# Filter rows interleaved over SBUF partitions, and x and the filter loaded by two queues on opposite halves

## The chip, the cores and the metric

The kernel runs on one core of a Trainium2 chip. The metric is the device time of one execution in microseconds; lower is better. An execution of the kernel before takes 2681.92 us (median of three, 2678.74 to 2682.32). "TensorE", "VectorE", "ScalarE", "GpSimd" (also POOL) and "SyncE" (also SP) are the core's engines; PE, PEld, DVE, ACT, POOL and SPq are their rows in the profile. DMAs are issued from SyncE, ScalarE (hardware queues) or GpSimd (the software queue).

## The reference

A spectral filter over the sequence axis, followed by a two-layer network with an ELU in between:

```python
batch, seq, dim = (8, 3008, 256)          # filt_r, filt_i: (1505, 256), float32
X = np.fft.rfft(x, axis=1)
F = (filt_r + 1j * filt_i)[None, :, :]
y = np.fft.irfft(X * F, n=x.shape[1], axis=1).astype(np.float32)

h = y.reshape(24064, 256) @ w_in          # w_in (256, 2048), double precision in DRAM
g = np.where(h > 0.0, h, np.exp(np.minimum(h, 0.0)) - 1.0)
out = (g @ w_out).astype(np.float32)      # w_out (2048, 256), double precision in DRAM
```

## The kernel before

The transform of length 3008 is split as 47 x 64. The first factor (64 points, `a_unit`, for batch 0 `a_first`) multiplies x by a twiddled table; the second (47 points, `b_unit`, L302) transforms over the other index with the tables `gb`/`gf` and multiplies by the filter on VectorE (L312 to L315); `bi_unit` (L325) goes back over the 47 points with `gr` and `gi`, `y_write`/`y_read` turn the layout through DRAM, and `n_unit` (L356) does the inverse 64 points and leaves the rows of y in SBUF. The network follows per group of rows: `up_steps` (h and the ELU, L411 to L433) and `down_steps` (L493), both by a scheme of seven products instead of eight.

The order is written out by hand (`tc.manual_schedule()`, L633): each engine executes its instructions, and each queue issues its DMAs, in program order. After a start-up for batch 0, a plan (L715 to L776) interleaves the network of one batch with the transforms of the next. The change lies in the start-up, and in the one-time arrangement of the filter in DRAM for batches 1 to 7.

The start-up has these parts:

- `w_fetch(k)`, k = 0 to 15 (L546): one 512 KB piece of the double-precision weights, on the GpSimd queue, into a borrowed buffer. `w_split` (VectorE), `w_float` (ScalarE) and `w_join` (VectorE) turn it into float32. `tick(k)` is `w_float(k)` and `w_join(k - 1)`.
- `x_load_first(c)`, c = 0 to 5 (L212): a twiddle table `tf` of 256 KB over 128 partitions, four rows per x position to partitions 0 to 63 (pieces of 4 KB), and the mirrored rows to partitions 64 to 127 (pieces of 1 KB). All three are on the sync queue.
- `a_first(c)` (L231) multiplies them and evicts to `zt`; `t_first(g)` (L246) transposes back.
- `f_read_first(ff, a, part)` (L280): the filter for batch 0 into `ff`, a tile of 128 partitions by 8 groups. Part 0 is `filt_r` on the sync queue, part 1 `filt_i` on the GpSimd queue; `a` is the half of the partitions (from 0, or from 64). In each half, rows 0 to 23 are the ascending frequencies (one transfer of 384 KB), rows 24 to 46 the mirrored ones, descending (each `u` in a transfer of 16 rows and one of 7, up to 128 and 56 KB). Row 24 to 47 of group 0 has one more transfer (L295).
- The loop over c (L667) splits, converts and joins weight c, runs `a_first(c)`, and fetches weight c + 2 once a one-element GpSimd copy (`junk`, L670) has seen x part c arrive.
- The loop over g = 0 to 9 (L688) is the filter stage: `b_unit` for group g, `bi_unit` and `y_write` for g - 2, and one weight by `TICKS`. At its end come the first `y_read` and `n_unit(0, 0)` (L711).

`f_arrange` (L615) later copies both filters into a DRAM tile `fd` whose rows lie as those of `ff`; `f_read` loads one group of it as 48 + 48 whole rows for the batches after the first.

Of the kernel before, what the change touches and what calls it, by code (L numbers as in the profile page):

```python
# [22 lines left out]
N1 = 47  # L23
# [17 lines left out]
def _make_tables():  # L41

    n2, k2 = np.arange(N2), np.arange(K2)
    ta, tn = np.zeros((P, H, P)), np.zeros((P, H, P))
    for i in range(H):
        for h in range(2):
            if h and i == 0:
                continue
            n1 = N1 - i if h else i
            th = 2 * np.pi * (((N1 * n2[:, None] + n1) * k2[None]) % N) / N  # L60
            c, s = np.cos(th), -np.sin(th)
            c[:, 0], s[:, 0] = 1.0, 1.0 - 2.0 * (n2 % 2)
            sign = -1.0 if h else 1.0
            r = slice(h * 64, h * 64 + 64)
            for p, v in enumerate((c, sign * s, s, sign * c)):
                ta[r, i, p * 32:p * 32 + 32] = v
                tn[p * 32:p * 32 + 32, i, r] = v.T
    tf = np.ascontiguousarray(ta.reshape(P, H, 4, K2).transpose(0, 1, 3, 2)).reshape(P, H, P)
    tb = ta.reshape(2, 2, 32, NXC, 2, 2, 4, 16, 2)[:, 0].transpose(3, 0, 1, 2, 4, 7, 5, 6)
    ta = np.ascontiguousarray(tb).reshape(P, H // 2, P)  # L70
    i = np.arange(H)[:, None]
    gb, gr, gi = (np.zeros((P, 2, 64)) for _ in range(3))
    q = np.arange(N1)[None]
    th = 2 * np.pi * ((i * np.where(q < 24, q, 70 - q)) % N1) / N1
    c, s = np.cos(th), np.sin(th)
    sign = np.where(q < 24, 1.0, -1.0)
    gb[0:24, 0, :N1], gb[24:48, 0, :N1] = c, s
    gb[64:88, 0, :N1], gb[88:112, 0, :N1] = c * sign, -s * sign
    for o in (0, 64):
        gr[o:o + N1, 0, 0:24], gr[o:o + N1, 0, 24:48] = 2 / N * c.T, 2 / N * s.T  # L80
        gi[o:o + N1, 0, 0:24], gi[o:o + N1, 0, 24:48] = 2 / N * (c * sign).T, -2 / N * (s * sign).T
    k1 = np.arange(24)[None]
    t0 = 2 * np.pi * ((i * k1) % N1) / N1
    t3 = 2 * np.pi * ((i * (32 + 64 * k1)) % N) / N
    c0, s0, c3, s3 = np.cos(t0), np.sin(t0), np.cos(t3), np.sin(t3)
    gb[0:24, 1, 0:24], gb[24:48, 1, 24:48] = c0, c3
    gb[64:88, 1, 24:48], gb[88:112, 1, 0:24] = -s3, -s0

    m0, m3 = np.full((24, 1), 2 / N), np.full((24, 1), 2 / N)
    m0[0] = m3[23] = 1 / N  # L90
    s0[:, 0] = s3[:, 23] = 0.0
    gr[0:24, 1, 0:24], gr[24:48, 1, 24:48] = m0 * c0.T, m3 * c3.T
    gi[0:24, 1, 24:48], gi[24:48, 1, 0:24] = -m0 * s0.T, -m3 * s3.T
    gf = np.zeros_like(gb)
    for o in (0, 64):
        gf[o:o + 48] = gb[o:o + 48].reshape(2, H, 2, 64).swapaxes(0, 1).reshape(48, 2, 64)
    return [t.astype(np.float32) for t in (ta, tn, gb, gr, gi, tf, np.eye(P), gf)]
# [8 lines left out]
def kernel(  # L106
# [39 lines left out]
    w_in, w_out = ([glob.tile([P, 7, 2, P], FP32, name="%s%d" % (n, i)) for i in range(4)] for n in ("wi", "wo"))  # L146

    fbufs = [glob.tile([P, 2, 2, D], FP32, name="f%d" % i) for i in range(FBUFS)]
    junk = glob.tile([P, 1], FP32, name="junk")
    edges = glob.tile([P, 2], FP32, name="edges")  # L150
    fd = fdp.tile([NG, 2, 48, 2, 2, D], FP32, name="fd")

# [2 lines left out]
    def raw(src, row, ap, col=0):  # L155
        return bass.AP(tensor=src.tensor, offset=src.offset + row * D + col, ap=ap)
# [52 lines left out]
    zt = [[], [w[3].rearrange("p a b c -> p (a b c)") for w in (w_in, w_out)]]  # L209
    ROWS = 112  # L210

    def x_load_first(c):  # L212
        if c < XBUFS:
            t = xp.tile([P, 2, 2, D], FP32, tag="xc", name="xc").rearrange("p k u d -> p (k u) d")
        else:
            t = t1p.tile([P, XC, D], FP32, tag="t1", name="x1")
        if c < 2:
            w = tnp.tile([P, 4, P], FP32, tag="tn", name="tn")
        else:
            if c % 2 == 0:  # L220
                tas["pair"] = t4p.tile([P, 4, D], FP32, tag="t4", name="t0").rearrange("p u (w f) -> p (u w) f", f=P)
            w = tas["pair"][:, 4 * (c % 2):4 * (c % 2) + 4, :]
        xs[0, c], tas[0, c] = t, w
        nc.sync.dma_start(w, tf_d[:, 4 * c:4 * c + 4, :])
        nc.sync.dma_start(t[HALVES[0]].rearrange("p u d -> p (u d)"), raw(x, XC * c, [[N1 * D, 64], [1, XC * D]]))
        u = 1 if c == 0 else 0
        if u:
            nc.gpsimd.memset(t[HALVES[1], 0, :], 0.0)
        nc.sync.dma_start(t[HALVES[1], u:XC, :], raw(x, N1 - XC * c - u, [[N1 * D, 64], [-D, XC - u], [1, D]]))

    def a_first(c):  # L231
        xt, w = xs.pop((0, c)), tas.pop((0, c))
# [44 lines left out]
        for a, r in enumerate((LO, HI)):  # L277
            nc.gpsimd.dma_start(t[r].rearrange("p c u d -> p (c u d)"), fd[g, a].rearrange("q c u d -> q (c u d)"))

    def f_read_first(t, a, part):  # L280

        r = a * 64
        for src, c, queue in (((filt_r, 0, nc.sync), (filt_i, 1, nc.gpsimd))[part],):
            queue.dma_start(t[r:r + 24, :, c, :, :].rearrange("q g u d -> q g (u d)"),
                                raw(src, 2 * a, [[64 * D, 24], [4 * D, NG], [1, 2 * D]]))
            for u in range(2):
                g0 = 1 if a == u == 0 else 0
                for r0, n in ((24, 16), (40, 7)):  # L290
                    queue.dma_start(t[r + r0:r + r0 + n, g0:NG, c, u, :],
                                        raw(src, 64 * (r0 - 23) - 4 * g0 - 2 * a - u,
                                            [[64 * D, n], [-4 * D, NG - g0], [1, D]]))
            if a == 0:
                queue.dma_start(t[24:48, 0, c, 0, :], raw(src, 32, [[64 * D, 24], [1, D]]))  # L295

    def tile_mm(ps, table, k, rhs, special):
        for u, w, v in ((0, 1, 1), (1, 1, 0)) if special else ((0, 2, 0),):
# [316 lines left out]
    def f_arrange():  # L615

        for c, src in enumerate((filt_r, filt_i)):
            for a in range(2):
                nc.gpsimd.dma_start(fd[:, a, 0:24, c, :, :].rearrange("g q u d -> q g (u d)"),
                                    raw(src, 2 * a, [[64 * D, 24], [4 * D, NG], [1, 2 * D]]))  # L620
                for u in range(2):
                    g0 = 1 if a == u == 0 else 0
                    nc.gpsimd.dma_start(fd[g0:NG, a, 24:47, c, u, :].rearrange("g q d -> q g d"),
                                        raw(src, 64 - 4 * g0 - 2 * a - u,
                                            [[64 * D, 23], [-4 * D, NG - g0], [1, D]]))

                g0 = 0 if a else 1
                nc.gpsimd.dma_start(fd[g0:NG, a, 47, c, :, :].rearrange("g u d -> g (u d)"),
                                    raw(src, 4, [[2 * D, NG - g0], [1, 2 * D]]))
            nc.gpsimd.dma_start(fd[0, 0, 24:48, c, 0, :], raw(src, 32, [[64 * D, 24], [1, D]]))  # L630
            nc.gpsimd.dma_start(fd[0, 0, 47:48, c, 1, :], raw(src, 4, [[D, 1], [1, D]]))

    with tc.manual_schedule():  # L633


        TICKS = {1: 8, 2: 9, 3: 10, 4: 11, 5: 12, 7: 13, 8: 14, 9: 15}
        with tc.tile_pool(name="boot", bufs=1) as bp:
            ff = bp.tile([P, NG, 2, 2, D], FP32, name="ff")
            eye = bp.tile([P, P], FP32, name="eye")
# [1 line left out]
            pq = [bp.tile([P, 2, D], FP32, name="pq%d" % i) for i in range(2)]  # L641
            zt[0] += [bp.tile([P, 16 * ROWS], FP32, name="zt%d" % i) for i in range(2)]

            for k in range(2):
                w_fetch(k)
            for c in range(NXC):
                x_load_first(c)
            wtmp.append([kp.tile([P, 512], U32, tag=t, name=n) for t, n in (("k0", "wm"), ("k1", "we"))] +
                        [kp.tile([P, 2, 512], FP32, tag="c", name="wfl")])
            wtmp.append([sdp.tile([P, 2, D], FP32, tag="sd", name=n).bitcast(U32).rearrange("p a b -> p (a b)")  # L650
# [1 line left out]
                        [t1p.tile([P, XC, D], FP32, tag="t1", name="wfl").rearrange("p (a b) d -> p a (b d)", a=2)])  # L652
            for i, v in enumerate((1151.0 * 2 ** 23, 255.0 * 2 ** 23)):
                nc.vector.memset(edges[:, i:i + 1], v)
            for z in zt[0] + zt[1]:
                nc.gpsimd.memset(z.rearrange("p (k r) -> p k r", r=ROWS)[:, :, 48:64], 0.0)
            nc.gpsimd.memset(ff, 0.0)
            for t, d in ((gr, gr_d), (gi, gi_d), (gf, gf_d), (eye, eye_d)):
                nc.sync.dma_start(t, d)
            for a in range(2):  # L660
                f_read_first(ff, a, 0)

            def tick(k):
                w_float(k)
                w_join(k - 1)

            for c in range(NXC):  # L667
                w_split(c)

                nc.gpsimd.tensor_copy(out=junk[0:1], in_=xs[0, c][0:1, 0, 0:1])  # L670
                w_fetch(c + 2)
                w_float(c)
                a_first(c)
                if c > 0:
                    w_join(c - 1)
            for a in range(2):
                f_read_first(ff, a, 1)
            for k in range(NXC + 2, 14):
                w_fetch(k)
            for g in range(4):  # L680
                t_first(g)
            for k in range(NXC, 8):
                w_split(k)
                tick(k)
                w_fetch(8 + k)
            nc.sync.dma_start(gb, gb_d)
            tn_read(0, 0)
            for g in range(NG + 2):  # L688
# [12 lines left out]
                    y_read(0, 0, (nc.sync, nc.scalar))  # L701
                if k:
                    tick(k)
        w_join(15)
        for c in range(2):
            x_load(1, c)
# [102 lines left out]
```

## Time and profile before

| What | Value |
|---|---|
| Time, median of three | 2681.92 us (2678.74 to 2682.32) |
| Span of the profiled execution | 2675.4 us |
| Busy share: PE, PEld, DVE, ACT, POOL | 97%, 83%, 69%, 56%, 9% |
| DMA rate, 0 to 30 us / 30 to 74 us | 235 / 192 GB/s, share of the DMA engines 0.97 / 1.02 |
| DVE busy, 0 to 30 / 30 to 74 / 74 to 126 us | 12.87 / 13.46 / 47.74 us |
| PE busy, 126 to 2675 us | 2533.72 of 2549 us |

The first row is from timed executions, the others from one profiled execution. The span is cut into stretches of time, and for each the busy time of every engine, the granted TensorE clock, the share of the 16 DMA engines that was occupied and the bytes per second are given. An engine that is full in a stretch bounds it; where none is and the DMA share is near 1, transfers do. In a timeline a row shows start, length, engine, line, operation, result and operands, and in brackets how long the engine was idle before it and what ended that.

### The profile page before, as it was taken

Reading aid. Unit: us, or ns where it says so; the run is one execution under the profiler, and the core shown is the slowest. Engines: PE = TensorE matmul, PEld = TensorE weight load, DVE = VectorE, ACT = ScalarE, POOL = GpSimd, SP = SyncE. Lnnn points to the kernel's source line nnn. Section 1 sums busy time; section 2 is a strip of 40 time slices with the busy share of each in tenths; the row PEclk is TensorE's granted clock in tenths of the full one; section 3 lists DMA queues with packets and bytes.
Section 4 is the critical chain, followed back from the end, with each engine's and each line's share of the span. In section 5 each row is a group of like instructions: output and inputs, shape, how many; then the busy total and the mean of one; then the engine's idle time right before and its main releaser. Section 6 shows DMA issues by size and latency. Waiting matters only on the chain.

```text
span 2675.4 us, 37291 instructions
## 1 busy us (share of the span) xinstructions
PE 2597.6 (97%) x13508; PEld 2213.8 (83%) x13508; DVE 1841.1 (69%) x3201; ACT 1504.4 (56%) x2621; POOL 252.2 (9%) x302
## 2 busy tenths in 40 slices
PE   3699999999999999999999999999999999999998
PEld 3388789887898878988789878898789887898887
DVE  3876766767766776767766776676767677666665
ACT  4565555655555555555555555555555555555554
POOL 3030200012000120002100021000210011000000
PEclk7799999999999999999999999999999999999999
DMA  9564421343114331343314233133421233110110
GB/s 194 145 143 100 112 50 38 90 104 97 38 45 120 86 85 35 82 104 79 77 43 102 73 97 75 38 85 97 103 56 38 73 83 85 38 40 19 22 26 16
DMA packets 230936, 202.87 MB, mean 76 GB/s; under 512 B 132952, under 2 KB 197579, under 8 KB 230753
## 3 DMA queue, kind: packets, MB, share of 16 engines
q1 hardware_dynamic: 213457, 164.84, 25.5%
q0 software_dynamic: 16992, 35.19, 5.5%
q8 instruction: 107, 1.75, 0.3%
q14 instruction: 76, 0.62, 0.1%
q10 hardware_dynamic: 304, 0.46, 0.1%
HBM read 128.45 MB, written 74.97 MB: 76 GB/s over the span
## 4 chain that ended last, share of the span: by engine, by line
PE 95%; DMA 3%; DVE 2%; ACT 0%; issue 0%; SPq 0%; POOL 0%; DVEq 0%; POOLq 0%; ACTq 0%
PE po L493 42%; PE phs L411 25%; PE phd L411 12%; PE pha L411 6%; PE psn L363 3%; PE pva L300 2%; PE psr L300 2%; PE psa L201 2%; DMA wd<-in_moe_w_out_dram 1%; DMA ff<-in_filt_i_dram 1%; DMA xc<-in_x_dram 1%; DMA tn<-tf_t 0%; PE pvb L300 0%; PE psa L236 0%; PE psi L300 0%
## 5 line engine op out<-in xcount | busy, mean ns | idle before, releaser
L493 PE MATMUL po<-g,wo 128*128 128x256 f32 (+1 forms) x5376 | 1297.1, 376 | 0.0
L493 PEld LDWEIGHTS po<-g,wo 128*128 128x128 f32 x5376 | 1016.7, 190 | 127.9 <-issue 16.2
L422 ACT ACTIVATE g<-phs 128x512 f32<-128x512 f32 (+1 forms) x576 | 338.7, 588 | 843.3 <-PE phs L411 842.6
L419 DVE TENSOR_TENSOR g<-phd,g 128x512 f32<-128x512 f32 (+1 forms) x384 | 259.4, 676 | 464.9 <-ACT e L429 278.7
L429 ACT ACTIVATE e<-e 128x512 f32<-128x512 f32 (+1 forms) x768 | 477.3, 621 | 24.3
L411 PE MATMUL phs<-y,wi 128*128 128x256 f32 (+1 forms) x1536 | 395.0, 380 | 0.0
L411 PE MATMUL phs<-ys,wi 128*128 128x256 f32 (+1 forms) x1536 | 387.8, 375 | 1.5 <-ACT g L422 1.5
L433 DVE SCALAR_TENSOR_TENSOR g<-e,g 128x512 f32<-128x512 f32 (+1 forms) x576 | 386.9, 672 | 0.2 <-ACT e L429 0.2
L428 ACT ACTIVATE e<-g 128x512 f32<-128x512 f32 (+1 forms) x576 | 352.9, 613 | 35.1 <-DVE g L419 29.0
L411 PEld LDWEIGHTS phs<-y,wi 128*128 128x128 f32 x1536 | 285.0, 190 | 82.7 <-ACT t L332 34.1
L411 PEld LDWEIGHTS phs<-ys,wi 128*128 128x128 f32 x1536 | 291.9, 190 | 34.8 <-ACT g L422 2.2
L433 DVE SCALAR_TENSOR_TENSOR g<-e,phs 128x512 f32<-128x512 f32 (+1 forms) x192 | 129.9, 677 | 138.4 <-ACT e L429 138.4
L411 PE MATMUL phd<-ys,wi 128*128 128x256 f32 (+1 forms) x768 | 194.0, 375 | 1.8 <-DVE g L419 1.8
L411 PE MATMUL pha<-y,wi 128*128 128x256 f32 (+1 forms) x768 | 193.9, 375 | 0.0
L411 PE MATMUL phd<-y,wi 128*128 128x256 f32 (+1 forms) x768 | 193.7, 375 | 0.0
L428 ACT ACTIVATE e<-phs 128x512 f32<-128x512 f32 (+1 forms) x192 | 112.9, 588 | 141.9 <-PE phs L411 141.0
L321 POOL TENSOR_TENSOR sr<-sr,sp 128x512 f32<-128x512 f32 x56 | 71.2, 1271 | 1242.8 <-DVE sp L314 1242.8
L411 PEld LDWEIGHTS phd<-ys,wi 128*128 128x128 f32 x768 | 145.9, 190 | 18.7 <-DVE g L419 2.5
L411 PEld LDWEIGHTS pha<-y,wi 128*128 128x128 f32 x768 | 146.0, 190 | 16.6 <-ACT y L365 0.2
L411 PEld LDWEIGHTS phd<-y,wi 128*128 128x128 f32 x768 | 146.1, 190 | 16.2
L473 DVE TENSOR_TENSOR g<-g,g 128x512 f32<-128x512 f32 (+1 forms) x192 | 130.7, 681 | 6.7
L470 DVE TENSOR_TENSOR g<-g,g 128x512 f32<-128x512 f32 (+1 forms) x192 | 130.7, 681 | 6.6
(141 smaller groups left out, 2403.0 us busy)
## 6 DMA issues: line engine op xcount, KB each, us to landing
yd<-t SPq DMA_DIRECT2D x127, 192.0 KB
t<-yd SPq DMA_DIRECT2D x190, 128.0 KB
z<-t SPq DMA_DIRECT2D x84, 256.0 KB
f<-fd POOLq DMA_DIRECT2D x112, 192.0 KB, 3.7
t<-z SPq DMA_DIRECT2D x224, 96.0 KB
out_dram<-o SPq DMA_DIRECT2D x640, 32.0 KB
tn<-tn_t SPq DMA_DIRECT2D x48, 256.0 KB
xc<-in_x_dram SPq DMA_DIRECT2D x84, 128.0 KB
```

The costliest lines, as they stand in the source:

```text
L300: nc.tensor.matmul(ps[:, u:u + w, :], table[k, v, :], r[k, u:u + w, :], start=n == 0, stop=n == len(rhs) - 1)
L321: nc.gpsimd.tensor_tensor(out=sr, in0=sr, in1=p, op=ALU.add)
L363: nc.tensor.matmul(ps[:, ts(q, P)], t[:, i - 4 * m, ds(dh * P, P)], w[:, i - 4 * m, :], start=True, stop=True)
L411: nc.tensor.matmul(ps[:, a, 0:h], w_in[q][:, COMBO[n], a, :], y[n], start=start and a == 0, stop=True, skip_group_check=True)
L419: nc.vector.tensor_tensor(out=g[o], in0=i0, in1=i1, op=ALU.add)
L422: nc.scalar.activation(out=g[o], in_=i0, func=AXT.Copy)
L428: nc.scalar.activation(out=e, in_=src, func=AXT.Relu, scale=-1.0)
L429: nc.scalar.activation(out=e, in_=e, func=AXT.Exp, scale=-1.0)
L433: nc.vector.scalar_tensor_tensor(out=g[n], in0=es[n], scalar=1.0, in1=src, op0=ALU.subtract, op1=ALU.max)
L470: nc.vector.tensor_tensor(out=b12, in0=b22, in1=b12, op=ALU.subtract)
L473: nc.vector.tensor_tensor(out=g["t4"], in0=g["b21"], in1=g["t2"], op=ALU.subtract)
L493: nc.tensor.matmul(po[i][:, u, 0:h], w_out[q][:, COMBO[n], a, :], g[n][:, a, :], start=q == 0 and a == 0 and n in (1, 3, 6, 4), stop=True, ...
```

## The change

It is meant to [...]keep two queues on opposite halves of the partitions at the same time. It has four parts:

1. In each half the filter's rows are interleaved: ascending frequencies on the even rows, mirrored ones on the odd rows. The rows and columns of the tables (`gb`, and with it `gf`, `gr`, `gi`) are permuted to fit, and so is the DRAM copy for the later batches.
2. x's upper rows go to the GpSimd queue, its lower rows and the twiddles stay on the sync queue. The filter's real part (sync) takes the lower half first, the imaginary part (GpSimd) the upper half first.
3. The order of the start-up: x and the weights 0 to 4 are issued in turn from the beginning, without the `junk` copies; the imaginary filter is issued after weight 6; weight 7 is converted in the filter stage at g = 0 and no longer ahead of it.
4. The zero fill of `ff` is split between ScalarE and VectorE, where GpSimd did it alone; that of one x row moves from GpSimd to VectorE.

```diff
@@ tables
+    lie = np.concatenate([2 * np.arange(24), 2 * np.arange(24) + 1])
+    gb[:, :, lie] = gb[:, :, :48].copy()
+    for t in (gr, gi):
+        for o in (0, 64):
+            t[o + lie] = t[o:o + 48].copy()
@@ x_load_first
         xs[0, c], tas[0, c] = t, w
-        nc.sync.dma_start(w, tf_d[:, 4 * c:4 * c + 4, :])
+        if c == 0:
+            nc.vector.memset(t[HALVES[1], 0, :], 0.0)
+
+    def x_load_first(c):
+        t = xs[0, c]
+        u = 1 if c == 0 else 0
         nc.sync.dma_start(t[HALVES[0]].rearrange("p u d -> p (u d)"), raw(x, XC * c, [[N1 * D, 64], [1, XC * D]]))
-        u = 1 if c == 0 else 0
-        if u:
-            nc.gpsimd.memset(t[HALVES[1], 0, :], 0.0)
-        nc.sync.dma_start(t[HALVES[1], u:XC, :], raw(x, N1 - XC * c - u, [[N1 * D, 64], [-D, XC - u], [1, D]]))
+        nc.gpsimd.dma_start(t[HALVES[1], u:XC, :], raw(x, N1 - XC * c - u, [[N1 * D, 64], [-D, XC - u], [1, D]]))
+        nc.sync.dma_start(tas[0, c], tf_d[:, 4 * c:4 * c + 4, :])
@@ f_read_first
-        for src, c, queue in (((filt_r, 0, nc.sync), (filt_i, 1, nc.gpsimd))[part],):
-            queue.dma_start(t[r:r + 24, :, c, :, :].rearrange("q g u d -> q g (u d)"),
...
+        src, queue = ((filt_r, nc.sync), (filt_i, nc.gpsimd))[c]
+        for a in ((0, 1), (1, 0))[c]:
+            r = a * 64
+            queue.dma_start(t[r:r + 48:2, :, c, :, :].rearrange("q g u d -> q g (u d)"),
...
-                for r0, n in ((24, 16), (40, 7)):
-                    queue.dma_start(t[r + r0:r + r0 + n, g0:NG, c, u, :],
...
+                for j, n in ((0, 16), (16, 7)):
+                    queue.dma_start(t[r + 1 + 2 * j:r + 2 * (j + n):2, g0:NG, c, u, :],
...
             if a == 0:
-                queue.dma_start(t[24:48, 0, c, 0, :], raw(src, 32, [[64 * D, 24], [1, D]]))
+                queue.dma_start(t[1:48:2, 0, c, 0, :], raw(src, 32, [[64 * D, 24], [1, D]]))
@@ f_arrange (its other transfers alike)
-                nc.gpsimd.dma_start(fd[:, a, 0:24, c, :, :].rearrange("g q u d -> q g (u d)"),
+                nc.gpsimd.dma_start(fd[:, a, 0:48:2, c, :, :].rearrange("g q u d -> q g (u d)"),
@@ start-up
-        TICKS = {1: 8, 2: 9, 3: 10, 4: 11, 5: 12, 7: 13, 8: 14, 9: 15}
+        TICKS = {0: 7, 1: 8, 2: 9, 3: 10, 4: 11, 5: 12, 7: 13, 8: 14, 9: 15}
...
-            for k in range(2):
-                w_fetch(k)
+            for z in zt[0] + zt[1]:
+                nc.gpsimd.memset(z.rearrange("p (k r) -> p k r", r=ROWS)[:, :, 48:64], 0.0)
+            for c in range(NXC):
+                x_place_first(c)
             for c in range(NXC):
                 x_load_first(c)
+                if c < 5:
+                    w_fetch(c)
+            nc.scalar.memzero(ff[:, 0:NG // 2])
+            nc.vector.memset(ff[:, NG // 2:NG], 0.0)
...
-            nc.gpsimd.memset(ff, 0.0)
...
-            for a in range(2):
-                f_read_first(ff, a, 0)
+            f_read_first(ff, 0)
...
             for c in range(NXC):
                 w_split(c)
-
-                nc.gpsimd.tensor_copy(out=junk[0:1], in_=xs[0, c][0:1, 0, 0:1])
-                w_fetch(c + 2)
                 w_float(c)
                 a_first(c)
                 if c > 0:
                     w_join(c - 1)
-            for a in range(2):
-                f_read_first(ff, a, 1)
-            for k in range(NXC + 2, 14):
+                    w_fetch(c + 4)
+                if c == 2:
+                    f_read_first(ff, 1)
+            for k in range(NXC + 4, 14):
                 w_fetch(k)
             for g in range(4):
                 t_first(g)
-            for k in range(NXC, 8):
-                w_split(k)
-                tick(k)
-                w_fetch(8 + k)
+            w_split(NXC)
+            tick(NXC)
+            w_fetch(14)
...
                 if k:
                     tick(k)
+                if g == 0:
+                    w_fetch(15)
```

More of the change, by code (lines that the diff above doesn't have):

```diff
@@ L148 @@
     fbufs = [glob.tile([P, 2, 2, D], FP32, name="f%d" % i) for i in range(FBUFS)]
-    junk = glob.tile([P, 1], FP32, name="junk")
     edges = glob.tile([P, 2], FP32, name="edges")
@@ L210, with x_place_first @@
     ROWS = 112
-    def x_load_first(c):
+    def x_place_first(c):
         if c < XBUFS:
@@ L278, in f_read, with f_read_first @@
             nc.gpsimd.dma_start(t[r].rearrange("p c u d -> p (c u d)"), fd[g, a].rearrange("q c u d -> q (c u d)"))
-    def f_read_first(t, a, part):
-        r = a * 64
-        for src, c, queue in (((filt_r, 0, nc.sync), (filt_i, 1, nc.gpsimd))[part],):
-            queue.dma_start(t[r:r + 24, :, c, :, :].rearrange("q g u d -> q g (u d)"),
-                                raw(src, 2 * a, [[64 * D, 24], [4 * D, NG], [1, 2 * D]]))
+    def f_read_first(t, c):
+        src, queue = ((filt_r, nc.sync), (filt_i, nc.gpsimd))[c]
+        for a in ((0, 1), (1, 0))[c]:
+            r = a * 64
+            queue.dma_start(t[r:r + 48:2, :, c, :, :].rearrange("q g u d -> q g (u d)"),
+                            raw(src, 2 * a, [[64 * D, 24], [4 * D, NG], [1, 2 * D]]))
             for u in range(2):
                 g0 = 1 if a == u == 0 else 0
-                for r0, n in ((24, 16), (40, 7)):
-                    queue.dma_start(t[r + r0:r + r0 + n, g0:NG, c, u, :],
-                                        raw(src, 64 * (r0 - 23) - 4 * g0 - 2 * a - u,
-                                            [[64 * D, n], [-4 * D, NG - g0], [1, D]]))
+                for j, n in ((0, 16), (16, 7)):
+                    queue.dma_start(t[r + 1 + 2 * j:r + 2 * (j + n):2, g0:NG, c, u, :],
+                                    raw(src, 64 * (j + 1) - 4 * g0 - 2 * a - u,
+                                        [[64 * D, n], [-4 * D, NG - g0], [1, D]]))
             if a == 0:
-                queue.dma_start(t[24:48, 0, c, 0, :], raw(src, 32, [[64 * D, 24], [1, D]]))
+                queue.dma_start(t[1:48:2, 0, c, 0, :], raw(src, 32, [[64 * D, 24], [1, D]]))
     def tile_mm(ps, table, k, rhs, special):
@@ L622, in f_arrange @@
                     g0 = 1 if a == u == 0 else 0
-                    nc.gpsimd.dma_start(fd[g0:NG, a, 24:47, c, u, :].rearrange("g q d -> q g d"),
+                    nc.gpsimd.dma_start(fd[g0:NG, a, 1:47:2, c, u, :].rearrange("g q d -> q g d"),
                                         raw(src, 64 - 4 * g0 - 2 * a - u,
@@ L629, in f_arrange @@
                                     raw(src, 4, [[2 * D, NG - g0], [1, 2 * D]]))
-            nc.gpsimd.dma_start(fd[0, 0, 24:48, c, 0, :], raw(src, 32, [[64 * D, 24], [1, D]]))
+            nc.gpsimd.dma_start(fd[0, 0, 1:48:2, c, 0, :], raw(src, 32, [[64 * D, 24], [1, D]]))
             nc.gpsimd.dma_start(fd[0, 0, 47:48, c, 1, :], raw(src, 4, [[D, 1], [1, D]]))
     with tc.manual_schedule():
-        TICKS = {1: 8, 2: 9, 3: 10, 4: 11, 5: 12, 7: 13, 8: 14, 9: 15}
+        TICKS = {0: 7, 1: 8, 2: 9, 3: 10, 4: 11, 5: 12, 7: 13, 8: 14, 9: 15}
         with tc.tile_pool(name="boot", bufs=1) as bp:
@@ L654 @@
                 nc.vector.memset(edges[:, i:i + 1], v)
-            for z in zt[0] + zt[1]:
-                nc.gpsimd.memset(z.rearrange("p (k r) -> p k r", r=ROWS)[:, :, 48:64], 0.0)
-            nc.gpsimd.memset(ff, 0.0)
             for t, d in ((gr, gr_d), (gi, gi_d), (gf, gf_d), (eye, eye_d)):
                 nc.sync.dma_start(t, d)
-            for a in range(2):
-                f_read_first(ff, a, 0)
+            f_read_first(ff, 0)
             def tick(k):
```

## The prediction

> **What bounds the kernel now.** I read the slices of the span first, then the windows, the timelines of VectorE and of the sync queue, the DMA queues by window, and last the chain of waits. The slices show the TensorE at 9 tenths everywhere but in the first two of 40, so the span is a start-up plus a steady stage at the speed of the matmuls:
>
> ```profile
> PE   3699999999999999999999999999999999999998
> ```
>
> The steady stage starts with the first spectral unit of the third factor (L363), at 125.49 us in the chain. From there to the end are 2675.4 - 125.5 = 2549.9 us in which the TensorE is 99% busy, and the diff touches almost nothing there. What can move is the first 125.5 us. The windows of the start-up (columns: us; busy time of PE, PEld, DVE, ACT, POOL with counts; TensorE clock; DMA share; GB/s):
>
> ```profile
> 20.00:25.00 5.00, 2.02 (x16) 1.86 (x16) 2.94 (x6) 2.97 (x7) 0.17 (x1) 1.00 1.05 274
> 30.00:35.00 5.00, 3.82 (x22) 3.60 (x20) 3.31 (x8) 3.92 (x11) 2.62 (x6) 0.72 1.07 255
> 40.00:45.00 5.00, 3.74 (x36) 3.60 (x40) 2.82 (x6) 3.67 (x9) 0.68 (x1) 1.00 0.97 151
> 55.00:60.00 5.00, 0.00 (x0) 0.00 (x0) 0.00 (x0) 0.00 (x0) 1.66 (x3) 0.50 0.93 127
> 60.00:65.00 5.00, 0.00 (x0) 0.00 (x0) 0.00 (x0) 0.00 (x0) 0.83 (x2) 0.50 1.08 132
> 70.00:75.00 5.00, 0.00 (x0) 0.00 (x0) 1.25 (x3) 0.47 (x1) 2.16 (x4) 0.50 1.01 370
> 85.00:90.00 5.00, 4.91 (x36) 1.91 (x33) 4.96 (x10) 4.60 (x9) 0.00 (x0) 1.00 0.32 77
> ```
>
> The reader is to see three things. Until 74 us the DMA engines are always occupied (share about 1), yet the bytes fall from about 255 GB/s to about 130 as soon as the filter is on the queues (35 to 65 us), and rise to 370 when only weights are left. From 55 to 65 us no compute engine does anything at all. After 75 us VectorE is full (4.96 of 5) and DMA idle. So there are two stretches, one bound by transfers and one by VectorE, and their seam is one wait on VectorE, before the first product with the filter:
>
> ```profile
> 73.75 0.69 DVE L312 TENSOR_TENSOR sr<-psr,ff 128x512 f32<-128x512 f32 x1 [23.22 <-DMA ff<-in_filt_r_dram]
> ```
>
> The sync queue's timeline says how long the real part of the filter was under way:
>
> ```profile
> 30.81 0.38 SPq L286 DMA_DIRECT2D ff<-in_filt_r_dram  x1
> 32.05 4.67 SPq L291 DMA_DIRECT2D ff<-in_filt_r_dram  x4
> 36.80 0.31 SPq L295 DMA_DIRECT2D ff<-in_filt_r_dram  x1
> 37.50 0.31 SPq L286 DMA_DIRECT2D ff<-in_filt_r_dram  x1
> 41.14 7.08 SPq L291 DMA_DIRECT2D ff<-in_filt_r_dram  x4
> ```
>
> First issue at 30.8, last bytes at 73.7: 43 us for 1.5 MB. Meanwhile the software queue fetched weights that nobody needed yet. The chain after the seam:
>
> ```profile
> 118.13 3.06 DMA yd<-t
> 121.64 3.72 DMA t<-yd
> 125.49 3.41 PE psn L363 x16
> ```
>
> [...]
>
> **The change part by part.** *Interleaved rows.* [...] The tables only permute; the products keep their shapes (48 rows, 64 columns), so PE and DVE cost the same. The copy in DRAM keeps its pieces of 1 and 2 KB; f_read is unchanged.
>
> *Queues.* x's upper rows go to the software queue, each followed by one weight fetch; the junk copies (0.17 to 0.72 us of POOL each, but 9.9 + 6.0 us of waits) go. The real filter stays on sync, lower half first; the imaginary one stays on POOL, upper half first, now issued after fetch 6 rather than after fetch 7. Bytes that must land before the first product:
> sync: x lower 1536 KB, twiddles 1536, four tables 256, filter 1505, together 4833 KB = 4.95 MB.
> POOL: x upper 1472, weights 0 to 6 at 512 each 3584, filter 1505, together 6561 KB = 6.72 MB, then weight 7 (0.52 MB), because w_split(7) now stands on VectorE ahead of the first product.
> Before, nearly all 15 weights beside them had moved by then (16.8 MB to 80 us). While both queues work I take 252 GB/s, the mean of the six windows from 5 to 35 us (262, 221, 245, 274, 258, 255), shared evenly: 9.9 MB take 39.3 us; with the rate up by 2.5 us (slices of the first 10 us), sync is done at 41.8. POOL then lacks 1.77 MB, its filter mostly, alone and on one half. The nearest rows are 10 to 20 us, when the sync queue alone moved 1.84 MB of x, half after half (184 GB/s), and the 127 of 55 to 60 us as the bad end. At 184: 9.6 us, to 51.4. Weight 7 at 370 GB/s: 1.4 us. The first product can start at 52.8.
>
> *Does compute allow that?* x's last upper part has 4.13 MB ahead on POOL with itself, at half of 252: 35 us. Weight 5 follows at 39.3; its four ScalarE rows (0.68 + 0.63 + 0.71 + 0.72 us) stand ahead of the last a_first evictions (4 x 0.38): 43.5. Before, from the last of these (40.33) to the filter unit's matmuls done (46) were 5.7 us: 49. This is below 52.8, so transfers still end last, by some 4 us.
>
> *After the seam.* Before: 73.75 to 118.13 is 44.4 us, VectorE without a gap over 0.6 us. Added: tick(7) at g = 0, which puts w_join(6) there (0.60 + 0.60 + 0.77 = 2.0 us at the rows of that stage). Weights 8 to 13 follow at 1.4 us each where VectorE needs one in five, so they hide. Then 7.4 us to the first L363 as before: 52.8 + 44.4 + 2.0 + 7.4 = 106.6 against 125.5, a gain of 18.9 us. The last ticks stand where they stood.
>
> *Memsets.* POOL loses the 6.92 us fill of ff. VectorE fills half: a fill of 1024 columns took 0.91 us (L776), so 3.6. ScalarE's zeroing has no row; by its copies of 512 (0.48 to 0.60 us), at most 4.8 us. Both lie before the first weights arrive (9.22 before, later now) and long before the filter: nothing. The fill of one x row moves from POOL to VectorE (0.3 us), hidden likewise. [...]nothing else in the start-up hangs on POOL.
>
> The time is 2681.9 - 18.9 = 2663.
>
> **Rivals.**
> (a) Interleaving moves nothing, because it is small packets[...] that are slow. Then 8.6 MB at 252 take 34 us and 3.1 MB at 127 take 24: with the start and weight 7 the seam is at 62, gain 9.7, time 2672. For it: [...]7-row reads stay small. Against: x's upper rows have pieces of 1 KB too and ran at about 230 to 250.
> (b) x on two halves at once runs at 300 or more: sync done at 35.5, filter at 250 GB/s to 42.6, weight 7 to 44; x and the transforms by the steps above (30, 33.5, 37.7) end at 43.4. With both this close a seam at 46: gain 25.7, time 2656. For it: 370 GB/s with all partitions. [...]
> (c) Slower: the software queue with x and all weights becomes the brake. At 50 to 60 us it moved 0.65 MB, 65 GB/s; at 85 GB/s its 6.72 MB take 79 us, with the start and weight 7 the seam is at 83, and the time 2681.9 + 83 - 73.75 + 2 = 2693. Against: it moved 1.04 MB in the first 10 us and 2.67 MB from 70 to 80.
> (d) No change: the seam lands at 66 to 77, when x phase and filter both keep the worst rates (8.6 MB at 220, 3.1 at 115: 39 + 27 + 4 = 70): 2680.
>
> **How the numbers follow.** Main case 0.57, (a) 0.17, (b) 0.12, (c) 0.06, (d) 0.08. The range goes from (b)'s time, 2656, to 2675, a seam at 65 us with main case and (a) inside. Faster is main, (a) and (b), 0.86; same (d), 0.08; slower (c), 0.06.
>
> **What would show it.** In the changed profile: the product at L312 starts near 53 instead of 73.75; GB/s in the filter's stretch stay above 180; no window without compute; 46 us from L312's start to the last y_write; the first L363 near 107; the steady stage again 2550 us. Wrong would be: a seam that waits for x or w rather than ff[...], a software queue below 100 GB/s, or a VectorE stretch longer than 47 us. If the steady stage changes by more than 3 us, I have missed a link.

## The result and the profile after

The changed kernel takes 2668.09 us (median of four, 2665.26 to 2669.53) against 2681.74 us (four executions in the same comparison, 2678.74 to 2682.32). The ratio is 0.995 with an interval of 0.9933 to 0.9967: it is faster, by 13.7 us by the medians. The same kernel, timed again later with more executions (14 of it, 51 of the kernel before), came to 0.9972 (0.9963 to 0.9981): 7.5 us by that ratio, 6.55 by the medians. The profiled executions differ by 2675.4 - 2667.6 = 7.8 us. The forecast was 18.9 us, so the sign is right and the size was overestimated, by more than half if the longer comparison is taken.

The slices of the changed kernel, TensorE's row. The start-up is still less than two slices long:

```profile
PE   4799999999999999999999999999999999999998
```

The windows of the changed kernel's start-up, with the columns of the table before (us; busy time of PE, PEld, DVE, ACT, POOL; clock; DMA share; GB/s):

```profile
20.00:25.00 5.00, 3.49 (x16) 3.49 (x16) 4.38 (x11) 3.74 (x10) 2.15 (x4) 0.50 1.05 289
30.00:35.00 5.00, 2.02 (x16) 1.86 (x16) 4.86 (x12) 4.40 (x10) 2.37 (x4) 1.00 1.08 269
40.00:45.00 5.00, 5.00 (x42) 4.05 (x40) 0.37 (x2) 4.23 (x9) 1.17 (x2) 0.79 1.03 158
55.00:60.00 5.00, 0.00 (x0) 0.00 (x0) 0.00 (x0) 0.53 (x1) 1.11 (x2) 0.50 1.05 292
60.00:65.00 5.00, 0.00 (x0) 0.00 (x0) 1.31 (x3) 0.00 (x0) 0.00 (x0) 0.50 0.75 271
70.00:75.00 5.00, 5.00 (x30) 2.15 (x29) 4.86 (x12) 3.19 (x6) 0.52 (x1) 0.72 0.24 58
```

Two things changed. The long trough of 121 to 132 GB/s is gone: 292 GB/s move from 55 to 60 us where 127 moved before. And yet VectorE and TensorE are idle there, as before, and VectorE's full stretch begins only after 63 us. The bytes flow, but they are not the ones that are waited for. VectorE's timeline, first the split of weight 7, then the first product with the filter:

```profile
52.96 0.43 DVE L584 TENSOR_SCALAR wm<-wd 128x512 uint32<-128x512 uint32 x1 [12.59 <-DMA wd<-in_moe_w_out_dram]
...
63.69 0.69 DVE L320 TENSOR_TENSOR sr<-psr,ff 128x512 f32<-128x512 f32 x1 [9.96 <-issue]
```

Weight 7 had landed at 52.96 us; the product came 10.7 us later. The bracket names no releaser, but the chain of waits runs through the real filter's transfers up to 53.73 us and then into 9.77 us that it can't attribute. The sync queue's timeline for these transfers:

```profile
21.62 0.95 SPq L294 DMA_DIRECT2D ff<-in_filt_r_dram  x1
24.07 7.45 SPq L299 DMA_DIRECT2D ff<-in_filt_r_dram  x4
32.36 0.77 SPq L303 DMA_DIRECT2D ff<-in_filt_r_dram  x1
34.46 0.80 SPq L294 DMA_DIRECT2D ff<-in_filt_r_dram  x1
37.50 12.21 SPq L299 DMA_DIRECT2D ff<-in_filt_r_dram  x4
```

The first is issued 9.2 us earlier than before (30.81), and the issue of the last ends 1.5 us later (49.7 for 48.2). From first issue to first product are 63.7 - 21.6 = 42.1 us, where the kernel before needed 73.75 - 30.81 = 42.9.

That looks as if only the start had moved, but an issue is not yet a transfer. The trace keeps every packet with its queue, start, length and size, and by size and order the real filter's pieces (384 of 2 KB, 737 of 1 KB) can be told from the others on the sync queue. The first starts at 32.1 us and the last ends at 62.8; in the kernel before it is 33.8 and 72.9. So the earlier issue brought the first bytes only 1.7 us earlier: four tables (256 KB in pieces of 512 bytes), issued ahead of them in the queue, went out only from 26 to 36 us, beside the weights and the imaginary filter of the software queue. What became shorter is the transfer itself, 30.7 us for 39.1. The imaginary filter was not the last: it was issued by 39.0 us, and none of its transfers took over 13.9 us to land.

What the engines carried meanwhile, by queue (packets, MB, share of the 16 engines), from 25 to 35 us:

```profile
q0 software_dynamic: 695, 2.22, 83.6%
q1 hardware_dynamic: 720, 0.49, 22.6%
```

And from 50 to 55 us:

```profile
q0 software_dynamic: 324, 1.12, 84.9%
q1 hardware_dynamic: 247, 0.25, 20.4%
```

The software queue, by then with weights only, moved 1.12 MB; the sync queue, with the last of the filter, 0.25 MB, or 50 GB/s. From 55 to 60 us it was 0.30 MB, by the sizes of the pieces 0.13 of the filter and 0.17 of two tables, `gb` and `tn`, that were issued behind it (49.75 and 51.16 us). After the seam nothing changed, as the chain shows:

```profile
110.01 3.06 DMA yd<-t
113.59 3.69 DMA t<-yd
117.36 3.55 PE psn L371 x16
```

From the first product to L371 (L363 before) are 53.7 us, and from there to the end 2667.6 - 117.4 = 2550.2 us, against 2549.9.

### The profile page after: what moved, and what is told of

Read it like the earlier page. It is cut to its first block, busy times and chain, and to the rows that moved or that the text cites. A ratio compares the mean times of both kernels' runs of the same rounds, so it can differ in the third digit from the quotient of the medians.

```text
span 2667.6 us, 37278 instructions
## 1 busy us (share of the span) xinstructions
PE 2597.2 (97%) x13508; PEld 2209.1 (83%) x13508; DVE 1843.3 (69%) x3203; ACT 1508.7 (57%) x2622; POOL 248.0 (9%) x300
## 4 chain that ended last, share of the span: by engine, by line
PE 94%; DVE 2%; DMA 2%; issue 1%; ACT 0%; SPq 0%; DVEq 0%
PE po L501 43%; PE phs L419 25%; PE phd L419 12%; PE pha L419 6%; PE psn L371 3%; PE pva L308 2%; PE psr L308 2%; PE psa L206 2%; DMA ff<-in_filt_r_dram 1%; DMA x<-in_x_dram 1%; DVE si L321 0%; DVE sr L320 0%; PE pvb L308 0%; DVE wfl L603 0%; DVE we L601 0%
## 5 line engine op out<-in xcount | busy, mean ns | idle before, releaser
L419 PEld LDWEIGHTS phd<-ys,wi 128*128 128x128 f32 x768 | 145.7, 190 | 18.9 <-DVE g L427 2.5
```

The lines of the kernel that those rows point to most:

```text
L419: nc.tensor.matmul(ps[:, a, 0:h], w_in[q][:, COMBO[n], a, :], y[n], start=start and a == 0, stop=True, skip_group_check=True)
```

## The experiments

The theory after the result: interleaved rows do shorten the filter's transfers, but the seam is set by the real filter's last pieces, which run beside the weights of the software queue and get the smaller part of the engines. The rivals: the gain comes from the queues alone and not from the rows; the last pieces are slow for themselves (their size, their addresses in DRAM, the partitions they go to); or the opposite halves matter.

The first stretch is not equally fast in all profiles (programs that are alike up to there issue the filter at 21.6 to 23.2 us, once at 19.8), so the table gives the span from first issue to first product too, and the time from the start of the real filter's first piece to the end of its last, by the packets. By that measure two profiles of one kernel agree within 0.5 us (30.7 and 30.5; 22.6 and 23.1). In filt_2k and filt_line the pieces can't be told by size. All times but the ratios are from one profiled execution each.

| Run | Real filter, first issue | First product | Span | First to last piece | First L363/L371 | Ratio to before (interval) |
|---|---|---|---|---|---|---|
| before | 30.8 | 73.75 | 42.9 | 39.1 | 125.5 | |
| after | 21.6 | 63.7 | 42.1 | 30.7 | 117.4 | 0.9950 (0.9933 to 0.9967) |
| after_again | 22.0 | 64.6 | 42.6 | 30.5 | 118.9 | 0.9972 (0.9963 to 0.9981) |
| rows_plain | 23.2 | 70.5 | 47.3 | 36.1 | 124.2 | 0.9993 (0.9985 to 1.0001) |
| rows_only | 31.8 | 69.7 | 37.9 | 33.4 | 124.1 | 0.9985 (0.9977 to 0.9992) |
| same_half | 22.7 | 63.6 | 40.9 | 29.5 | 117.5 | 0.9975 (0.9964 to 0.9985) |
| x_sync | 44.0 | 69.8 | 25.8 | 21.9 | 123.6 | 0.9996 (0.9988 to 1.0005) |
| weights_behind | 19.8 | 55.6 | 35.8 | 22.6 | 109.8 | 0.9943 (0.9929 to 0.9956) |
| weights_behind_b | 22.8 | 60.0 | 37.2 | 23.1 | 114.3 | 0.9950 (0.9935 to 0.9965) |
| weights_behind7 | 22.3 | 57.4 | 35.1 | 22.2 | 112.0 | 0.9954 (0.9937 to 0.9970) |
| weights_1k | 23.2 | 62.1 | 38.9 | 26.0 | 116.0 | 0.9952 (0.9938 to 0.9965) |
| filt_2k | 22.4 | 64.6 | 42.2 | | 118.4 | 0.9953 (0.9938 to 0.9968) |
| filt_line | 22.0 | 59.8 | 37.8 | | 113.8 | 0.9960 (0.9944 to 0.9975) |
| filt_act | 5.7 | 68.1 | 62.4 | 33.5 | 122.4 | 0.9987 (0.9980 to 0.9993) |

Runs after_again, rows_only, weights_behind_b and filt_act share one set of executions of the kernel before, as do rows_plain, weights_behind, weights_1k and filt_2k, and same_half, filt_line, x_sync and weights_behind7. Comparisons within such a set are the firmer ones.

**The changed kernel once more.**

> The changed kernel as it is, beside the others of this call, so that they can be compared with it on one chip: ratio to before 0.995, seam at 62 to 65 us.

The seam was at 64.6 us, as expected. The ratio was 0.9972, with an interval that only just overlaps the first one's. The 0.995 that was expected lies outside it. The first comparison rests on four executions of each kernel; this one is narrower, and the first pair of profiles (7.8 us) sides with it.

**Old rows under the new queues** (rows_plain):

```diff
-            queue.dma_start(t[r:r + 48:2, :, c, :, :].rearrange("q g u d -> q g (u d)"),
+            queue.dma_start(t[r:r + 24, :, c, :, :].rearrange("q g u d -> q g (u d)"),
...
-                    queue.dma_start(t[r + 1 + 2 * j:r + 2 * (j + n):2, g0:NG, c, u, :],
+                    queue.dma_start(t[r + 24 + j:r + 24 + j + n, g0:NG, c, u, :],
```

> The changed kernel with the filter's rows (and the tables and the DRAM copy) back in their old order, the queues as changed. If the interleaving[...] brought the gain, [...]the seam, 63.7 us in the changed profile, falls back to 70 or later: about 2676 us. If the gain came from the earlier start of the real filter on the sync queue (21.6 us instead of 30.8), nothing moves: seam 62 to 66, 2668 us within 3.

VectorE's timeline of this run, the first product:

```profile
70.49 0.69 DVE L315 TENSOR_TENSOR sr<-psr,ff 128x512 f32<-128x512 f32 x1 [10.35 <-issue]
```

The seam falls back to 70.5 us and the gain is gone (0.9993). The source rows, the bytes, the order and the queues are the same; only the partitions that the pieces go to differ. So the interleaving is worth 6 to 7 us at the seam (70.5 against 64.6 and 63.7, in other sets) and 5.5 us from first to last piece (36.1 for 30.6), and the rival that gives it nothing falls.

**Interleaved rows alone, in the kernel before** (rows_only): the rows, tables and DRAM copy of the change, nothing else.

> The kernel before with the filter's rows interleaved and nothing else. With the old rows under the new queues the ratio was 0.9993, with x back on the sync queue 0.9996: either part alone left nothing. If the two parts need each other, the filter's last transfers still end behind the weights here, the seam stays at 70 to 74 and the ratio at 0.998 to 1.000. If the rows save[...] for themselves (7 us between the seams with and without them), the seam comes to 66 to 68 and the ratio to 0.997.

```profile
69.69 0.69 DVE L317 TENSOR_TENSOR sr<-psr,ff 128x512 f32<-128x512 f32 x1 [18.49 <-DMA ff<-in_filt_r_dram]
```

The span from first issue to first product is 37.9 us instead of 42.9: the rows save 5 us for themselves, without the queues (5.7 from first to last piece, 33.4 for 39.1). The seam comes 4 us earlier, between the two forecasts (66 to 68, or 70 to 74), and the ratio, 0.9985, is a clear but small gain. In the profile 2.6 of the 4 us are lost after the seam (first product to L363 54.4 us for 51.7), where VectorE waits 2.25 us for psi at one place.

**x's upper rows back on the sync queue** (x_sync): one word in `x_load_first`, `nc.gpsimd` to `nc.sync`.

> The changed kernel with x's upper rows back on the sync queue. If the earlier start of the real filter (21.6 us instead of 30.8) is what the queue split brings, it starts at 27 to 30 us here and the seam falls back by 3 to 6 us, ratio about 0.997. If only the sum of bytes[...] decide, POOL is free earlier by as much, and the seam moves by less than 2 us: ratio 0.995.

The sync queue's first filter transfer and VectorE's first product:

```profile
44.02 0.94 SPq L294 DMA_DIRECT2D ff<-in_filt_r_dram  x1
...
69.78 0.69 DVE L320 TENSOR_TENSOR sr<-psr,ff 128x512 f32<-128x512 f32 x1 [14.78 <-DMA ff<-in_filt_r_dram]
```

The real filter starts at 44.0 us, much later than expected: the software queue now runs ahead with weights and the imaginary filter, and x, all on sync, crawls beside it (sync 0.92 MB, software queue 1.32 from 25 to 35 us; the last products of x at 49.09 us, 30.25 in the changed kernel). The gain is gone (0.9996). Under the new order, without the waits on x that the `junk` copies were, the split of x is therefore needed. But once the filter is under way it takes only 25.8 us, most weights being in already, and the imaginary filter too (its last issue is at 32.6 us). That is the first sign that the 42 us are not the filter's own.

**Both queues on the same half** (same_half): `for a in (0, 1)` for both parts.

> The changed kernel with the imaginary filter taken in the same order of halves as the real one (from partition 0, then from 64), so that both queues write the same half at a time. If the opposite halves matter, [...]the seam, 63.7 us in the changed profile, falls back by 3 to 6 us: ratio to before about 0.997. If each transfer is slow for itself, nothing moves: ratio 0.995.

```profile
63.58 0.69 DVE L320 TENSOR_TENSOR sr<-psr,ff 128x512 f32<-128x512 f32 x1 [7.75 <-issue]
```

Seam 63.6, ratio 0.9975, beside 63.7 and 64.6 of the changed kernel and its 0.9972: the opposite halves bring nothing that can be seen. The ratio alone would have spoken for them (0.997 was forecast if they matter); it is the seam, and the changed kernel's own 0.9972 in a later set, that speak against.

**Weights behind the filter** (weights_behind, and once more beside the changed kernel as weights_behind_b):

```diff
-            nc.gpsimd.dma_start(wd[:, ts(i, n), :].rearrange("p a w -> p (a w)"), s)
+            (nc.gpsimd if k < 7 else nc.sync).dma_start(wd[:, ts(i, n), :].rearrange("p a w -> p (a w)"), s)
```

> The changed kernel with weights 7 to 15 on the sync queue behind the real filter, so that no weight fetch runs beside its last transfers. If the sync queue's 1 KB pieces starve beside the software queue's 2 and 4 KB weight pieces (50 to 60 GB/s against 230 from 50 to 60 us), both filters are in by 48 to 50 us, weight 7 two later, the seam at 50 to 54 and the time about 2657. If the last transfers are slow[...], the seam stays at 60 or later and the time at 2664 to 2668.

> The changed kernel with weights 7 to 15 on the sync queue behind the real filter, once more beside the changed kernel. If the real filter's last pieces are held back by the weights' larger packets, its seam is 5 to 8 us earlier than that of the changed kernel in this call and the ratio 0.992 to 0.993. If the difference seen was one of the chip, both agree within 2 us.

The second run's DMA queues from 50 to 52.5 us (the real filter alone) and from 50 to 55 us, then VectorE's timeline:

```profile
q1 hardware_dynamic: 280, 0.33, 67.6%
q1 hardware_dynamic: 543, 0.71, 87.7%
```

```profile
59.36 0.43 DVE L584 TENSOR_SCALAR wm<-wd 128x512 uint32<-128x512 uint32 x1 [17.30 <-DMA wd<-in_moe_w_out_dram]
...
60.04 0.68 DVE L320 TENSOR_TENSOR sr<-psr,ff 128x512 f32<-128x512 f32 x1
```

The 0.71 MB are not the filter's alone: weight 7, issued behind it in the same queue at 51.37 us, has 0.26 MB of them. The filter's own bytes in these 5 us are 0.45 MB, for 0.24 and 0.31 in the two profiles of the changed kernel. Its last piece ends at 57.1 us for 63.7 (6.6 us earlier), and from first to last piece it takes 23.1 us for 30.5; the seam comes 64.6 - 60.0 = 4.6 us earlier in the one set, 8.1 us across sets. Both are short of what was expected (the first run between its two forecasts, the second just under 5 us and with 0.9950 for 0.992 to 0.993). Ratio 0.9950 (0.9935 to 0.9965) against 0.9972 (0.9963 to 0.9981) in the same set: faster than the changed kernel by some 6 us by the medians (2663.67 for 2670.21), with intervals that touch. It is the fastest version of its set. What ends last has changed too: not the filter, but weight 7 behind it, at 59.36 us. The run moves more than the weights, though: `gb` and `tn`, which followed the filter in the sync queue, now come behind weights 7 to 14 (62.53 and 63.19 us). How much of the gain is theirs was not separated; weights_1k below, which leaves them in place, shows that the weights have a part.

**Weight 7 back on the software queue** (weights_behind7): `k < 8` for `k < 7`.

> As the run with weights 7 to 15 behind the real filter on the sync queue, but weight 7 stays on the software queue behind the imaginary filter, since in that run VectorE waited last for weight 7 (54.93 us), not for the filter. Expected: weight 7 in by 48 us, the seam where the filter lands, between 49 and 54; the time 2 to 5 us below that run, ratio 0.992 to 0.994. If the filter itself lands at 55, no gain over it: 0.9943.

```profile
57.38 0.69 DVE L320 TENSOR_TENSOR sr<-psr,ff 128x512 f32<-128x512 f32 x1 [3.75 <-DMA ff<-in_filt_r_dram]
```

Now the filter ends last again, 35.1 us after its first issue, against 42.1 and 42.6. The first forecast, a seam at 49 to 54 us, failed; the second came true: no gain over weights_behind can be seen (0.9954; 0.9943 and 0.9950). From first to last piece the real filter takes 22.2 us, as in weights_behind (22.6 and 23.1), so one weight beside it costs nothing that shows.

**Weights in small pieces** (weights_1k):

```diff
+                for h in range(n // 128):
+                    nc.gpsimd.dma_start(wd[:, ds(n * i + 128 * h, 128), :].rearrange("p a w -> p (a w)"), s[:, ts(h, 256)])
```

> The changed kernel with weights 7 to 15 fetched in pieces of 1 KB instead of 2 and 4, on the same queue in the same order. If the engines take turns between the queues by packets, equal pieces give the sync queue about half of the bytes beside them, and the real filter lands some 4 us earlier: seam 58 to 60, time about 2663. If the turns are by bytes[...], the seam stays at 63 to 64 or is later[...]: 2668 to 2672.

The queues from 50 to 55 us in this run:

```profile
q0 software_dynamic: 207, 0.54, 49.8%
q1 hardware_dynamic: 411, 0.46, 42.1%
```

The seam moved to 62.1 us, between the two forecasts, and the span to 38.9 (26.0 us from first to last piece), and the sync queue got 0.46 MB where it got 0.25, as expected. But it doesn't show turns by packets: the software queue's packets were 0.54 MB / 207 = 2.6 KB on average, not 1 KB (3.5 KB before), so pieces were put together, and GpSimd, with two to four times the issues, sent less (0.54 MB for 1.12). Less traffic beside the filter explains it as well.

**The filter in pieces of 2 KB** (filt_2k), **and from one place in DRAM** (filt_line). Each half and part is one transfer of 48 rows. Neither kernel applies the right filter: the mirrored frequencies aren't read as such, in the second run all values are in other places. The bytes are about the same:

```diff
+            queue.dma_start(t[r:r + 48, :, c, :, :].rearrange("q g u d -> q g (u d)"),
+                            raw(src, 2 * a, [[31 * D, 48], [4 * D, NG], [1, 2 * D]]))
```

and for filt_line

```diff
-                            raw(src, 2 * a, [[31 * D, 48], [4 * D, NG], [1, 2 * D]]))
+                            raw(src, 737 * a, [[16 * D, 48], [2 * D, NG], [1, 2 * D]]))
```

> The changed kernel with the filter of batch 0 read by one transfer of 48 rows for each half and part, all in pieces of 2 KB; the mirrored frequencies are thereby not read as such, the bytes are about the same (768 KB for 752 a half). If each piece has a large fixed cost, half as many pieces halve the filter's time beside the weights: seam 50 to 55, time about 2658. [...]

> As the run with one 48-row transfer for each half and part (seam 64.6 us, 129 to 159 GB/s from 35 to 50 us), but every partition reads 16 KB that lie together in DRAM (rows 0 to 767 and 737 to 1504 of each part; the filter values are thereby in the wrong places). If the scattered reads in DRAM hold the filter back, the rate in that stretch rises to 230 or more and the seam comes to 55. If the writes into SBUF do, both stay: seam 63 to 66.

The windows from 40 to 45 us, of filt_2k and then of filt_line:

```profile
40.00:45.00 5.00, 2.45 (x12) 2.48 (x13) 1.87 (x5) 1.09 (x2) 0.54 (x1) 0.50 1.05 129
```

```profile
40.00:45.00 5.00, 5.00 (x31) 4.89 (x30) 1.08 (x3) 3.52 (x7) 0.54 (x1) 0.65 1.06 139
```

Neither helps the rate in that window: 129 and 139 GB/s, for 158 in the changed kernel. Larger pieces alone therefore don't mend it (span 42.2 for 42.1); these rows lie in one block of 48, so the run changes their place as well, and the number of transfers. For the scattered reads it stays open: the rate rises to 222 GB/s only from 45 us on and the seam is 4.8 us earlier than in filt_2k, which neither side had expected; the ratios (0.9953, 0.9960) do not show it.

**The real filter on a third queue from the start** (filt_act): as weights_behind, with `nc.scalar` for `filt_r`.

> As weights_behind, but the real filter is issued on the ScalarE queue right after the zero fill, at about 6 us, so that its small pieces are under way beside x and the weights from the start. If what slows the filter is its writes[...], they now run beside transfers[...], and the sum of the bytes sets the seam: 48 to 52 us, ratio 0.990 to 0.992. If its pieces only take the place of x's, the last transform of x comes later by as much and the seam stays at 55 or later.

ScalarE's timeline:

```profile
5.69 1.42 ACTq L294 DMA_DIRECT2D ff<-in_filt_r_dram  x1
11.37 22.36 ACTq L299 DMA_DIRECT2D ff<-in_filt_r_dram  x4
...
40.79 0.66 ACT L590 ACTIVATE wfl<-f 128x512 f32<-128x512 uint32 x1 [35.13 <-issue]
```

A plain miss: 0.9987. The small filter transfers were not issued in one go (four took 22.36 us); ScalarE stood between them, and its first conversion came at 40.79 us instead of 10.22. From 5 to 35 us this third queue moved 0.69 MB while the two others moved 3.95 and 2.68 MB. Here a queue that belongs to an engine with work cost that engine's time, 35.13 us without a conversion. The real filter was in by 45.1 us, but VectorE's first product then waited for the products of the late transforms (2.65 us for psi). Whether the filter beside x would have been cheap was not tested by it.

## Why the prediction was right, and where it was too high

- **What bounds the kernel, and where the change acts: right.** The steady stage kept its length (2550.2 for 2549.9 us) and the whole difference is in the seam. Of the signs it named, the 46 us after the seam and the steady stage came true; a product near 53 us, over 180 GB/s throughout (158 from 40 to 45 us) and no window without compute did not.
- **After the seam: right.** Forecast 46.4 us to the last y_write and 53.8 to the first L363; measured 110.01 - 63.69 = 46.3 and 53.7. The tick moved into the stage cost its 2 us.
- **Memsets: right.** ScalarE's zeroing took 3.62 us, VectorE's 3.47, both over before 6 us, the first weight's split at 10.22.
- **Compute allows it: right.** The filter unit's products were done by about 45.5 us (49 forecast), and did not end last.
- **The rate and the bytes: about right.** The windows from 5 to 35 us have 279, 294, 290, 289, 272 and 269 GB/s, 282 in the mean for the assumed 252. Up to 50 us the windows add up to 11.9 MB (5 us times a sum of 2387 GB/s); the forecast's sum for both queues without weight 7 was 11.67 MB, due at 51.4 us. Weight 7 was due at 52.8 us and was split at 52.96. That agreement is partly luck: the software queue was to be alone from 41.8 us at 184 GB/s, a rate read where the other queue moved another 0.50 MB (10 to 20 us of the kernel before). In fact the real filter ran beside it until 62.8 us.
- **The sharing: wrong, and the miss arose there.** The step that failed is "shared evenly" and what followed from it, "POOL then lacks 1.77 MB, its filter mostly, alone". It was the sync queue that came last: its 4.95 MB were due at 41.8 us and were complete at 62.8. The sharing was uneven long before the filter's end: from 25 to 35 us, when the sync queue sent the last twiddles, its four tables and the first of the filter, it moved 0.49 MB beside 2.22. By 50 us the software queue had moved 7.35 MB, of which 6.72 were needed, and the sync queue 4.56. By the time the right number of bytes had moved, the software queue had thus sent weights that belonged after the seam, and part of the real filter was still to come, at 50 GB/s beside 224 (0.25 and 1.12 MB in 5 us). The seam came 63.7 - 52.8 = 10.9 us late; 18.9 - 10.9 = 8.0 us is the gain of the profiles (7.8). Holding the weights back returned 4.6 us of it in the same set (weights_behind_b) and made weight 7 the next thing waited for. What the rest is stays open; even alone the real filter moved only 133 GB/s (50 to 52.5 us of weights_behind_b), where 184 had been taken for the other queue's remainder.
- **The interleaved rows: a gain, for a reason that was not shown.** How much the rows would shorten the transfers, and why, was the author's estimate, which no trace of the kernel before showed; the seam of 52.8 us was worked out from bytes and rates without it. Measured from first to last piece: 5.7 us by the rows alone in the kernel before (39.1 to 33.4), 5.5 us under the new queues (36.1 to 30.6). Rival (a), no effect of the rows, fell with rows_plain. rows_plain differs from the changed kernel only in the partitions that the pieces go to, so that is where the 5.5 us lie; what about the partitions makes the difference was not shown.
- **Opposite halves: no effect that can be seen** (same_half: seam 63.6 us, for 63.7 and 64.6).
- **Luck.** The seam of 63.7 us lies nearer to rival (a)'s 62 than to the main case's 52.8, and so does the longer comparison's gain (6.55 to 7.5 us, for 9.7 and 18.9). The time fell into a range that had been drawn to hold (a) as well. Yet (a)'s reason, that the rows do nothing, is refuted by rows_plain and rows_only.
- **How the parts add up.** By the ratios: rows alone 0.15%, queues and order alone (rows_plain) 0.07%, which can't be told from nothing, both 0.28%, all with intervals of about 0.08 either way. They roughly add; the larger part is the rows. From first to last piece the rows save 5.7 us under the old queues and 5.5 under the new, so each part does its own work whether or not the other is there; the queues and order save some 3.

Why the engines give the sync queue so little beside the weights stays open. So does how each transfer of 24, 16 or 7 rows is spread over the 16 engines: no view splits the packets by engine, and no run isolates it. From 50 to 60 us of the changed kernel the packets of the two queues are near in number (660 and 528) and four to one in bytes (2.28 and 0.55 MB), which would fit turns by packets, but weights_1k did not isolate it, and in filt_act the third queue got fewer packets than the others too (532 beside 1163 and 1370, 5 to 35 us).

## What to carry to other kernels

Here the sum of the bytes told when enough had moved (11.9 MB by 50 us), not when the transfer that was waited for ended (62.8 us): ask what else sits in the other queue beside the last piece that is waited for, and put what is not needed yet behind it, in the same queue (4.6 us at the seam, weights_behind_b, `gb` and `tn` moved with the weights). An earlier issue was not an earlier transfer (9.2 us at the issue, 1.7 us at the first bytes): look at what stands ahead in the same queue, small tables too (256 KB here). Which partitions a transfer writes mattered at equal bytes and equal rows (5.5 us of 36), so try narrow transfers on interleaved rows. And time a change of 0.3% with many executions: four gave 0.50%, fourteen 0.28%.

## What was not expected of the hardware

- Small pieces on a hardware queue sank to 50 GB/s beside weight fetches on the software queue that moved 224 (50 to 55 us of the changed kernel, DMA share 1.05).
- 256 KB of tables in pieces of 512 bytes, issued from 12.9 us on, went out only from 26 to 36 us, and the filter, issued behind them at 21.6 us, started only at 32.1 (changed kernel).
- The real filter alone moved only 133 GB/s and occupied the engines to 68% (weights_behind_b, 50 to 52.5 us); weights alone moved 395 (60 to 65 us, share 1.04).
- ScalarE computed nothing from 5.7 to 40.8 us while it issued eleven transfers to its own queue (filt_act).
